# Batch 0 of a fused attention and maxout-FFN kernel: fillers between the turns, and another order for the first loads

## The chip, the cores and the metric

The kernel runs on one core of a Trainium2 chip. The metric is the device time of one execution in microseconds, a median over several executions. The kernel before was run again beside each group of variants, on the same chip. A ratio is the mean time of one kernel's runs over the mean of the other's runs in the same rounds, so it is not quite the ratio of the medians that I quote. Each execution also reports its mean granted TensorE clock.

## The reference, cut to what matters

```python
k_all = np.concatenate([beacon_k, k], axis=2)      # B = H = 8, S = 576, D = 64, 16 beacons
v_all = np.concatenate([beacon_v, v], axis=2)
scores = scale * np.matmul(q, k_all.transpose(0, 1, 3, 2))
scores = np.where(causal, -1000000000.0, scores)
a = softmax(scores)
attn = np.matmul(a, v_all)
x = attn.transpose(0, 2, 1, 3).reshape(B * S, H * D)          # 4608 x 512
h = np.maximum(np.maximum(x @ w1, x @ w2), x @ w3)            # 512 x 768 each
out = h @ w_out
```

## The kernel before

TensorE executes a fixed order of work. A *pair* is two heads, a *quad* four heads; batch 0 has pairs 0 to 3. For each pair q and k are *turned* (transposed on TensorE into PSUM and copied back by VectorE), then scores are computed in four groups, ScalarE takes the exponential, VectorE or GpSimd masks it, and TensorE multiplies it with the values. The FFN is cut into units of matmuls that are interleaved with the attention of the next batch. The first twelve units need weights 1 and 2 only, and the thirteenth is the first that needs weight 3.

The first batch is written out as a list of steps; each entry is a group of scores and what follows it:

```python
first_steps = [
    ((0, 0), [T(2, 0, False)]),                      # T(p, h): turn half h of pair p
    ((1, 0), [T(3, 0, True, None, 4), L(next_load, 2), V(0)]),
    ((2, 0), []),
    ((3, 0), [T(0, 1, False, None, 4), M(0, 0, True), V(1), L(load_w, 0, 0, d_ff), V(2)]),
    ...
    ((0, 2), [T(2, 1, False), M(2, 0, True), M(0, 2), V(3), V(4), L(load_w, 1, 0, d_ff)]),
    ((0, 3), [T(3, 1, False), M(3, 0, True), M(0, 3, True)]),
    ((1, 1), [M(1, 1)]),
    ...
    ((2, 2), [P(1, 0, True, 2, 4), invert_sums, M(2, 2, True), G(0), L(load_wide, n_quad, 1)]),
    ((2, 3), [P(0, 1, False, 0, 2), multiply, M(2, 3), CW(2, 0), L(load_w, 2, 0, d_ff)]),
    ((3, 1), [P(0, 1, False, 2, 4), invert_sums, F(1), M(3, 1, True)]),     # F: one FFN unit
    ...
    ((3, 3), [F(1), M(3, 3, True), CW(2, 1), L(turn_quad, 2, 0), F(1), TW(2, 1, 0), P(1, 1), ...]),
]
```

`load_w(i, ...)` loads weight i + 1 in two pieces, issued by GpSimd, with a cast to bf16 on the way. `G(0)` and `load_wide(n_quad, 1)` load q and k of the first quad of batch 1 through SyncE's queue; G's load waits for a tiny VectorE memset into its buffer, which is how it is held back until VectorE has got that far (in the profile of the kernel before the memset runs at 22.11 us for 0.06 and the load goes out at 22.19). `CW` casts a loaded quad on GpSimd. `keep_busy` and `fill` issue matmuls or transposes whose result nobody reads; they only occupy TensorE:

```python
def fill(ps, n):
    for i in range(n):
        x0 = 512 + 128 * (i % 4)
        nc.tensor.transpose(ps[:, x0 : x0 + 128], busy[:, 0:128], ident)

def keep_busy(n, cols=320, ffn=False):
    ps = ffn_psum.tile([128, 512], FP32, name="fps") if ffn else pv_bank(1, [128, 512], FP32)
    for _ in range(n):
        nc.tensor.matmul(ps[:, 0:cols], busy[:, 0:128], busy[:, 0:cols], start=True, stop=True)
```

The softmax here doesn't subtract the row's maximum and nothing guards it: scores larger than these inputs give would overflow.

Of the kernel before, what the change touches and what calls it, by code (L numbers as in the profile page):

```python
# [16 lines left out]
def kernel(  # L17
# [13 lines left out]
    nc = tc.nc  # L31
# [5 lines left out]
    d_model, d_ff = moe_w1.shape  # L37
# [26 lines left out]
    n_quad = 2  # L64
# [5 lines left out]
    B_PE = 4  # L70
# [71 lines left out]
    bk16_1 = const.tile([NB_PE - Nb, H, D], BF16, name="bk16_1")  # L142
# [21 lines left out]
    def pv_bank(i, shape, dtype):  # L164
        return pv_psum.tile(shape, dtype, name=f"pv{i}")
# [3 lines left out]
    by_pool = nc.gpsimd.tensor_copy  # L169
# [217 lines left out]
    def fill(ps, n):  # L387

        for i in range(n):
            x0 = 512 + 128 * (i % 4)  # L390
            nc.tensor.transpose(ps[:, x0 : x0 + 128], busy[:, 0:128], ident)

    def turn_half(p, h, pv, q_copy=None, idle=0):
        for i in range(2):
            src = stage.pop(("half16", p, h, i))
            if pv:
                bank = pv_bank(i, [128, 1024], BF16)
            else:
                bank = ffn_psum.tile([128, 1024], BF16, name="fps")
            ps = bank[:, 0:HALF]  # L400
            if i == 0:
                fill(bank, idle)
            for r in range(HR):
                for e in range(2):
                    nc.tensor.transpose(
                        ps[64 * e : 64 * e + 64, r * QP : (r + 1) * QP],
                        src[:, e, r],
                        ident[0:QP, 0:QP],
                        tile_position=(0, 64 * e),
                    )  # L410
            x0 = i * Nb + HALF * h
            dst = (qTs, kTs)[i][p % NT][:, x0 : x0 + HALF]
            (q_copy if i == 0 and q_copy else by_dve)(  # L413
                dst.rearrange("d (p r) -> d p r", r=HR), ps.rearrange("d (r p) -> d p r", r=HR)
            )
# [272 lines left out]
    def emit_ffn(limit, pool=None, name="fps"):  # L688
        if done[0] == len(units):
            return False  # L690
        need, fn, args = units[done[0]]
        if done[0] + 1 <= limit + 1e-6 and need <= ready[0]:
            fn(*args, pool or ffn_psum, name)
            done[0] += 1
            return True
        return False
# [5 lines left out]
    def at_step(p, g, *fns):  # L702
        plan.setdefault((p, g), []).extend(fns)

    def L(fn, *a):
        return lambda: fn(*a)
# [3 lines left out]

    def load_qk(b):
        if b < B_PE:
            return [L(load_wide, n_quad * b + g, i) for g in range(n_quad) for i in range(2)]
        return [L(load_pair, p) for p in range(b * PPB, (b + 1) * PPB)]

    loads = [L(load_v, 0, 0, nc.gpsimd), L(load_v, 0, 1, None, (nc.scalar, nc.sync)), L(load_beacons, 1, B_PE, bk32_1)]
    loads += load_qk(1)[2:] + load_v_pieces(1)
    for b in range(2, B):
        if b == B_PE - 1:
            loads.append(L(load_beacons, B_PE, B, bk32))  # L720
        loads += load_qk(b) + load_v_pieces(b)

    def next_load(n=1):
        for _ in range(n):
            if loads:
                loads.pop(0)()

    def C(fn, *a):
        def run():
            fn(*a)  # L730
            next_load()

        return run

    def start():
# [22 lines left out]
        cast_half(0, 1, by_act)  # L758
        by_dve(bk16_0, bk32_0)
        turn_half(0, 0, False, by_act)  # L760
        keep_busy(4)
        turn_beacons(0, 1, bk16_0)
        by_act(qk_all[:, 1:PPB, S : S + Nb], bT[:, 1:PPB, 0:Nb])
        cast_half(1, 0, by_dve)
        cast_half(1, 1, by_dve)
        keep_busy(2)
        turn_half(1, 0, True, by_act)

    pv_at = {}
# [4 lines left out]
    def steps(p):  # L774
        return [[0, 1], [2, 3]]

    def T(p, h, pv, q_copy=None, idle=0):
        def run():
            turn_half(p, h, pv, q_copy, idle)

        return run

    def M(p, gi, dve=False):
        return L(emit_masks, p, gi, dve)

    def P(quad, hf, apart=False, first=0, last=len(passes)):
        return L(emit_pv, quad, hf, first, last, apart)

    def V(t):
        return L(cast_first_v, t)  # L790

    def G(i):
        return L(load_wide, n_quad, i, nc.vector)

    def F(n):
        return lambda: [emit_ffn(END) for _ in range(n)]

    def CW(quad, i):
        return L(cast_wide, quad, i, by_pool)

    def TW(quad, i, n, act=False):
        return L(turn_wide, quad, i, n, by_act if act else by_dve, False)

    def cast_p():
        for g in range(n_quad):
# [6 lines left out]

    first_steps = [
        ((0, 0), [T(2, 0, False)]),
        ((1, 0), [T(3, 0, True, None, 4), L(next_load, 2), V(0)]),
        ((2, 0), []),
        ((3, 0), [T(0, 1, False, None, 4), M(0, 0, True), V(1), L(load_w, 0, 0, d_ff), V(2)]),
        ((0, 1), [T(1, 1, True), M(1, 0, True), M(0, 1)]),
        ((0, 2), [T(2, 1, False), M(2, 0, True), M(0, 2), V(3), V(4), L(load_w, 1, 0, d_ff)]),
        ((0, 3), [T(3, 1, False), M(3, 0, True), M(0, 3, True)]),  # L820
        ((1, 1), [M(1, 1)]),
        ((1, 2), [P(0, 0, False, 0, 2), M(1, 2)]),
        ((1, 3), [P(0, 0, False, 2, 4), invert_sums, M(1, 3, True)]),
        ((2, 1), [P(1, 0, True, 0, 2), multiply, M(2, 1), cast_p]),
        ((2, 2), [P(1, 0, True, 2, 4), invert_sums, M(2, 2, True), G(0), L(load_wide, n_quad, 1)]),
        ((2, 3), [P(0, 1, False, 0, 2), multiply, M(2, 3), CW(2, 0), L(load_w, 2, 0, d_ff)]),
        ((3, 1), [P(0, 1, False, 2, 4), invert_sums, F(1), M(3, 1, True)]),
        ((3, 2), [F(1), multiply, L(turn_beacons, 1, B_PE, bk16_1), L(next_load, 5), M(3, 2, True)]),
        ((3, 3), [F(1), M(3, 3, True), CW(2, 1), L(turn_quad, 2, 0), F(1), TW(2, 1, 0), P(1, 1), invert_sums, TW(2, 1, 1, True),
                  L(place_quad_beacons, 2, by_act), F(1), multiply]),  # L830
    ]
    at_step(4, 0, C(cast_wide, 3, 0, by_pool))
    at_step(4, 1, C(cast_wide, 3, 1, by_pool))
    at_step(5, 0, C(cast_v, 1, 0, by_pool))
    at_step(5, 1, C(cast_v, 1, 1, by_pool))
    at_step(5, 0, L(load_w_out))
# [3 lines left out]
    for b in range(2, B):  # L840
        p = b * PPB
# [6 lines left out]
    for b in range(B_PE, B):  # L848
        p = b * PPB
# [117 lines left out]
```

## Time and profile before

| | kernel before |
|---|---|
| median of the first three runs | 300.07 us (299.07 to 300.17) |
| span of the profiled execution | 298.3 us |
| TensorE busy | 286.5 us |
| TensorE at half clock | 15.73 to 25.97 us |
| first quad of batch 1 requested | 22.19 us |
| first scores of batch 1 | 36.02 us |

Idle time of TensorE is what to look for, since it is busy 96% of the span; but "busy" does not tell at which clock, so the clock row has to be read beside it. The lines themselves stand in the prediction.

### The profile page before, as it was taken

The page shows a single profiled execution, that of the slowest core. Times are in us where ns is not written, and L with a number is a line of the kernel's source. Part 1 is how long each engine was busy: PE and PEld are TensorE (multiplying, and loading weights), DVE is VectorE, ACT ScalarE, POOL GpSimd, SP SyncE. Part 2 cuts the span into 40 slices and gives each one's busy share as a digit, 9 for nine tenths or more (in the row PEclk, how much of TensorE's full clock was granted, in tenths as well). Part 3 has the DMA queues.
Part 4 walks back from the last instruction along what each step waited for, and adds up shares of the span by engine and source line. Part 5 has one row for each costly group of instructions (what it writes and reads, how often), then busy time and mean ns, then how long its engine had stood idle before and what let it go on. Part 6 is the DMA issues. An engine that isn't in the chain of part 4 may idle for free.

```text
span 298.3 us, 8565 instructions
## 1 busy us (share of the span) xinstructions
PE 286.5 (96%) x3548; PEld 153.2 (51%) x3548; DVE 173.8 (58%) x341; ACT 147.3 (49%) x231; POOL 121.7 (41%) x241
## 2 busy tenths in 40 slices
PE   8699899999999999999999999999999999999995
PEld 4446675454545445454545777545454554444442
DVE  3754766456667565646563757375746575284373
ACT  4775488776655455546453646364635431401300
POOL 7282298465446453636454645554233210000000
PEclk9957999999999999999999999999999999999999
DMA  8999999977927999999999899898412001103003
GB/s 146 212 177 322 234 279 270 195 266 203 226 54 206 213 254 224 191 195 239 265 190 237 226 234 223 207 208 201 117 69 79 2 0 73 70 3 122 18 0 141
DMA packets 83589, 50.64 MB, mean 170 GB/s; under 512 B 64224, under 2 KB 75232, under 8 KB 83552
## 3 DMA queue, kind: packets, MB, share of 16 engines
q1 hardware_dynamic: 77904, 45.50, 65.1%
q0 software_dynamic: 4048, 4.03, 8.4%
q10 hardware_dynamic: 1600, 0.59, 1.0%
q8 instruction: 27, 0.44, 0.7%
q14 instruction: 10, 0.08, 0.1%
HBM read 35.13 MB, written 14.22 MB: 165 GB/s over the span
## 4 chain that ended last, share of the span: by engine, by line
PE 87%; DVE 5%; ACT 3%; DMA 2%; issue 1%; POOL 1%; POOLq 0%; DVEq 0%
PE fps L596 32%; PE pv L536 14%; PE sc L596 12%; PE fps L632 11%; PE sc L464 10%; PE sc L632 4%; PE fps L615 2%; DMA quad<-in_k_dram 2%; ACT at_sb L473 1%; PE pv L373 1%; DVE qkT L380 1%; DVE at_sb L490 1%; DVE xT L568 1%; DVE y L640 1%; DVE qkT L413 1%
## 5 line engine op out<-in xcount | busy, mean ns | idle before, releaser
L473 ACT ACTIVATE at_sb<-sc 128x928 bf16<-128x928 f32 (+5 forms) x128 | 104.0, 861 | 88.3 <-PE sc L464 86.5
L596 PE MATMUL fps<-xT,w_sb 128*128 128x512 bf16 (+1 forms) x488 | 110.2, 357 | 0.5 <-DVE xT L568 0.5
L492 POOL TENSOR_SCALAR_AFFINE_SELECT at_sb<-at_sb 128x256 bf16<-128x256 bf16 (+2 forms) x146 | 53.2, 383 | 105.7 <-ACT at_sb L473 105.0
L596 PEld LDWEIGHTS <-w_sb 128*128 128x128 bf16 x672 | 61.6, 98 | 65.0 <-issue 12.0
L606 DVE TENSOR_TENSOR hT<-hT,fps 128x512 bf16<-128x512 bf16 x72 | 49.4, 687 | 34.4 <-PE fps L596 34.4
L596 PE MATMUL sc<-xT,w_sb 128*128 128x512 bf16 (+1 forms) x184 | 42.1, 356 | 0.0
L464 PE MATMUL sc<-qkT 64*128 64x288 bf16 (+5 forms) x400 | 36.6, 284 | 2.3 <-ACT at_sb L473 0.7
L632 PE MATMUL fps<-w_out_sb,hT 128*128 128x512 bf16 x150 | 36.0, 379 | 0.0
L640 DVE COPY y<-fps 128x512 f32<-128x512 f32 x25 | 17.3, 692 | 27.6 <-PE fps L632 24.8
L632 PEld LDWEIGHTS <-hT 128*128 128x128 bf16 x210 | 19.8, 98 | 24.0 <-DVE hT L606 1.9
L536 PE MATMUL pv<-at_sb,v_sb 128*32 128x288 bf16 (+5 forms) x1376 | 30.3, 235 | 0.4 <-issue 0.4
L606 DVE TENSOR_TENSOR hT<-hT,sc 128x512 bf16<-128x512 bf16 x30 | 20.6, 688 | 16.4 <-PE sc L596 16.2
L604 DVE CAST hT<-fps 128x512 bf16<-128x512 f32 x31 | 21.4, 692 | 12.8 <-PE fps L596 12.8
L568 DVE TENSOR_TENSOR xT<-pv,recip 128x288 bf16<-128x288 f32 (+2 forms) x93 | 27.3, 349 | 2.6 <-ACT recip L558 2.6
L464 PEld LDWEIGHTS <-qkT 64*128 64x128 bf16 x400 | 14.4, 95 | 26.3 <-issue 18.9
L536 PEld LDWEIGHTS <-v_sb 128*32 128x32 bf16 (+1 forms) x1408 | 25.4, 99 | 3.9 <-issue 2.2
L248 POOL CAST p<-st 96x768 bf16<-96x768 f32 x32 | 25.5, 823 | 0.0
L287 POOL CAST v_sb<-st 128x1536 bf16<-128x1536 f32 (+2 forms) x21 | 18.4, 895 | 0.0
L536 PE MATMUL pv<-at_sb,ones 128*32 128x288 bf16 (+4 forms) x500 | 17.7, 263 | 0.4 <-DVE qkT L380 0.4
L556 ACT ACTIVATE lnd<-pv 128x288 f32<-128x288 f32 x31 | 12.9, 416 | 8.5 <-PE pv L536 8.5
L237 POOL CAST p<-st 128x1152 bf16<-128x1152 f32 x12 | 13.7, 1143 | 5.1 <-DMA st<-in_q_dram 5.1
L604 ACT CAST hT<-sc 128x512 bf16<-128x512 f32 x6 | 3.5, 585 | 23.7 <-PE sc L596 23.7
(73 smaller groups left out, 173.9 us busy)
## 6 DMA issues: line engine op xcount, KB each, us to landing
out_dram<-y SPq DMA_DIRECT2D x35, 256.0 KB, 2.3
st<-in_v_dram SPq DMA_DIRECT2D x23, 256.0 KB, 6.5
st<-in_q_dram SPq DMA_DIRECT2D x16, 288.0 KB, 4.6
st<-in_k_dram SPq DMA_DIRECT2D x16, 288.0 KB, 5.3
st<-in_q_dram SPq DMA_DIRECT2D x6, 576.0 KB, 6.3
st<-in_k_dram SPq DMA_DIRECT2D x6, 576.0 KB, 6.9
w_sb<-in_moe_w_dram POOLq DMA_DIRECT2D x6, 384.0 KB, 6.6
q_dram<-p SPq DMA_DIRECT2D x16, 144.0 KB, 2.3
```

The costliest lines, as they stand in the source:

```text
L248: cast(part.rearrange("p r h d -> p h r d"), st[0:QP, i * NQ2 : (i + 1) * NQ2].rearrange("p (h r d) -> p h r d", h=2, r=QR),)
L287: cast(v_sb[0:n, t:t1].rearrange("p t h d -> p (t h d)"), st[0:n, (t - t_lo) * H * D : (t1 - t_lo) * H * D],)
L464: nc.tensor.matmul(ps[:, e, off : off + q1 - q0], kT[hs, 128 * t : 128 * t + 128], qT[hs, q0:q1], start=True, stop=True, tile_position=(64 ...
L473: nc.scalar.activation(out=both_heads(p, gi), in_=ps[:, :, 0 : g_width(p, gi)], func=AF.Exp, scale=scale)
L492: nc.gpsimd.affine_select(out=view, in_=view, compare_op=ALU.is_ge, fill=0.0, base=x0, pattern=[[0, 2], [1, hi - lo]], channel_multiplier=-1,)
L536: nc.tensor.matmul(ps[bank][32 * j : 32 * j + 32, lo + q0 - qa : lo + qb - qa], lhsT, at_view(pair_of(quad, j)[0], t, pair_of(quad, j)[1], ...
L568: nc.vector.tensor_mul(xT[:, 2 * g + part - 1, c0 + ca : c0 + cb], ps[bank][:, lo : lo + cb - ca], recip[:, ca:cb],)
L596: nc.tensor.matmul(ps[:, o0 : o0 + n], w_in[i][:, ct, 128 * ft : 128 * (ft + 1)], xT[:, ct, x0 : x0 + n], start=(ct == 0), stop=(ct == n_c ...
L604: (by_act if alone[0] else by_dve)(h, ps)
L606: nc.vector.tensor_max(h, h, ps)
L632: nc.tensor.matmul(ps, hT[:, ft, 128 * tt : 128 * (tt + 1)], w_out_sb[:, ft, :], start=(ft == 0), stop=(ft == n_ft - 1),)
L640: nc.vector.tensor_copy(y, ps)
```

## The change

Its intent, as far as the code tells it: spread a few fillers over the gaps between the turns so that TensorE's clock stays up; move the last turn of pair 3 behind the scores (1,1); ask for the first quad of batch 1 two groups of scores sooner and ahead of weight 2; hold the second quad back until VectorE has passed a certain mask; and request weight 3 last, behind the casts of the second quad. The core of the diff:

```diff
-            if i == 0:
-                fill(bank, idle)
+            fill(bank, idle[i])
...
-            return [L(load_wide, n_quad * b + g, i) for g ... for i in range(2)]
+            return [L(load_wide, n_quad * b + g, i, nc.vector if (b, g, i) == (1, 1, 0) else None) for g ... for i in range(2)]
...
-        ((2, 0), []),
+        ((2, 0), [L(keep_busy, 1, 320, True)]),
...
+        ... V(2), L(keep_busy, 1)]),                                   # end of (3, 0)
-        ((0, 2), [T(2, 1, False), M(2, 0, True), M(0, 2), V(3), V(4), L(load_w, 1, 0, d_ff)]),
-        ((0, 3), [T(3, 1, False), M(3, 0, True), M(0, 3, True)]),
-        ((1, 1), [M(1, 1)]),
+        ((0, 2), [T(2, 1, False, None, (0, 3)), M(2, 0, True), M(0, 2), V(3), V(4)]),
+        ((0, 3), [M(0, 3, True), L(keep_busy, 1)]),
+        ((1, 1), [T(3, 1, False), M(3, 0, True), M(1, 1)]),
...
+        ((1, 3), [..., M(1, 3, True), G(0), L(load_wide, n_quad, 1)]),
+        ((2, 1), [..., M(2, 1), L(load_w, 1, 0, d_ff), cast_p]),
-        ((2, 2), [..., M(2, 2, True), G(0), L(load_wide, n_quad, 1)]),
-        ((2, 3), [..., M(2, 3), CW(2, 0), L(load_w, 2, 0, d_ff)]),
...                                          # in (3, 3): TW(2, 1, 0) now ahead of the FFN unit
-    at_step(4, 1, C(cast_wide, 3, 1, by_pool))
+    at_step(4, 1, C(cast_wide, 3, 1, by_pool), L(load_w, 2, 0, d_ff))
```

More of the change, by code (lines that the diff above doesn't have):

```diff
@@ L391, in fill, with turn_half @@
             nc.tensor.transpose(ps[:, x0 : x0 + 128], busy[:, 0:128], ident)
-    def turn_half(p, h, pv, q_copy=None, idle=0):
+    def turn_half(p, h, pv, q_copy=None, idle=(0, 0)):
         for i in range(2):
@@ L712, in load_qk @@
         if b < B_PE:
-            return [L(load_wide, n_quad * b + g, i) for g in range(n_quad) for i in range(2)]
+            return [L(load_wide, n_quad * b + g, i, nc.vector if (b, g, i) == (1, 1, 0) else None) for g in range(n_quad) for i in range(2)]
         return [L(load_pair, p) for p in range(b * PPB, (b + 1) * PPB)]
@@ L775, in steps, with T @@
         return [[0, 1], [2, 3]]
-    def T(p, h, pv, q_copy=None, idle=0):
+    def T(p, h, pv, q_copy=None, idle=(0, 0)):
         def run():
@@ L814 @@
         ((0, 0), [T(2, 0, False)]),
-        ((1, 0), [T(3, 0, True, None, 4), L(next_load, 2), V(0)]),
-        ((2, 0), []),
-        ((3, 0), [T(0, 1, False, None, 4), M(0, 0, True), V(1), L(load_w, 0, 0, d_ff), V(2)]),
+        ((1, 0), [T(3, 0, True, None, (4, 0)), L(next_load, 2), V(0)]),
+        ((2, 0), [L(keep_busy, 1, 320, True)]),
+        ((3, 0), [T(0, 1, False, None, (4, 0)), M(0, 0, True), V(1), L(load_w, 0, 0, d_ff), V(2), L(keep_busy, 1)]),
         ((0, 1), [T(1, 1, True), M(1, 0, True), M(0, 1)]),
-        ((0, 2), [T(2, 1, False), M(2, 0, True), M(0, 2), V(3), V(4), L(load_w, 1, 0, d_ff)]),
-        ((0, 3), [T(3, 1, False), M(3, 0, True), M(0, 3, True)]),
-        ((1, 1), [M(1, 1)]),
+        ((0, 2), [T(2, 1, False, None, (0, 3)), M(2, 0, True), M(0, 2), V(3), V(4)]),
+        ((0, 3), [M(0, 3, True), L(keep_busy, 1)]),
+        ((1, 1), [T(3, 1, False), M(3, 0, True), M(1, 1)]),
         ((1, 2), [P(0, 0, False, 0, 2), M(1, 2)]),
-        ((1, 3), [P(0, 0, False, 2, 4), invert_sums, M(1, 3, True)]),
-        ((2, 1), [P(1, 0, True, 0, 2), multiply, M(2, 1), cast_p]),
-        ((2, 2), [P(1, 0, True, 2, 4), invert_sums, M(2, 2, True), G(0), L(load_wide, n_quad, 1)]),
-        ((2, 3), [P(0, 1, False, 0, 2), multiply, M(2, 3), CW(2, 0), L(load_w, 2, 0, d_ff)]),
+        ((1, 3), [P(0, 0, False, 2, 4), invert_sums, M(1, 3, True), G(0), L(load_wide, n_quad, 1)]),
+        ((2, 1), [P(1, 0, True, 0, 2), multiply, M(2, 1), L(load_w, 1, 0, d_ff), cast_p]),
+        ((2, 2), [P(1, 0, True, 2, 4), invert_sums, M(2, 2, True)]),
+        ((2, 3), [P(0, 1, False, 0, 2), multiply, M(2, 3), CW(2, 0)]),
         ((3, 1), [P(0, 1, False, 2, 4), invert_sums, F(1), M(3, 1, True)]),
-        ((3, 2), [F(1), multiply, L(turn_beacons, 1, B_PE, bk16_1), L(next_load, 5), M(3, 2, True)]),
-        ((3, 3), [F(1), M(3, 3, True), CW(2, 1), L(turn_quad, 2, 0), F(1), TW(2, 1, 0), P(1, 1), invert_sums, TW(2, 1, 1, True),
+        ((3, 2), [F(1), multiply, L(turn_beacons, 1, B_PE, bk16_1), M(3, 2, True), L(next_load, 5)]),
+        ((3, 3), [F(1), M(3, 3, True), CW(2, 1), L(turn_quad, 2, 0), TW(2, 1, 0), F(1), P(1, 1), invert_sums, TW(2, 1, 1, True),
                   L(place_quad_beacons, 2, by_act), F(1), multiply]),
```

## The prediction

What (a) calls a filler net of the drain is measured in the kernel before: one filler of 320 columns at full clock lasts 0.299 us and two together 0.45, so the second adds 0.15 (these are the warm ones; the twelve ahead of 4.4 us last 0.474 each, in the median); one filler transpose lasts 0.22 and four 0.40, so each further one adds 0.06. That the fillers would keep the clock was my estimate from the busy times of the windows. The windows are 3.41 us long, a third of the two measured stretches of 10.24. The "near 400 GB/s" of (f) is the 392 of the last window; that weight 3 would share that rate was an estimate.

> **What bounds the kernel now.** I read the page first, for busy shares and clock. Its columns are forty slices of 7.46 us, in tenths.
>
> ```profile
> PE 286.5 (96%) x3548; PEld 153.2 (51%) x3548; DVE 173.8 (58%) x341; ACT 147.3 (49%) x231; POOL 121.7 (41%) x241
> ...
> PE   8699899999999999999999999999999999999995
> ...
> PEclk9957999999999999999999999999999999999999
> DMA  8999999977927999999999899898412001103003
> ```
>
> TensorE is the bound: 286.5 of 298.3 us busy, so only 12 us idle, and the waits of TensorE after 36 us list nothing above 0.7 us in total. Work that TensorE gets through earlier at the start should therefore come off the end. The change touches only the first 45 us. There the page shows two faults: a second slice with 6 tenths busy, and a third and fourth slice whose clock is 5 and 7 tenths.
>
> Second, I read windows cut where the clock changes (us, busy time by engine, clock, DMA share, GB/s):
>
> ```profile
> 5.49:8.90 3.41, 2.79 (x48) 1.66 (x47) 2.36 (x7) 1.98 (x6) 0.54 (x1) 1.00 1.44 201
> 8.90:12.31 3.41, 2.44 (x48) 1.53 (x48) 1.89 (x6) 2.96 (x3) 0.61 (x1) 1.00 1.40 185
> 12.31:15.73 3.42, 2.36 (x46) 1.54 (x48) 3.30 (x13) 2.32 (x3) 2.08 (x4) 1.00 1.33 229
> 15.73:19.14 3.41, 3.41 (x58) 1.51 (x54) 2.17 (x8) 2.62 (x4) 2.88 (x7) 0.50 1.06 194
> 19.14:22.55 3.41, 3.41 (x64) 1.59 (x66) 1.24 (x6) 2.74 (x5) 2.30 (x6) 0.50 1.00 170
> 22.55:25.97 3.42, 3.42 (x78) 2.29 (x71) 0.89 (x3) 1.93 (x4) 0.33 (x1) 0.50 1.00 249
> 25.97:29.38 3.41, 3.41 (x34) 2.22 (x32) 2.15 (x6) 2.12 (x5) 0.72 (x1) 1.00 1.04 392
> ```
>
> The clock falls to one half at 15.73 us and returns at 25.97: 10.24 us. Before the fall TensorE was busy 2.79, 2.44 and 2.36 us per 3.41 us, falling; then, at half clock, it is busy all the time and everybody waits for it.
>
> Third, I read the timelines of each engine around the hand-over to batch 1 (28 to 36 us) and before the fall:
>
> ```profile
> 14.12 0.32 PE L405 MATMUL fps<-ident,quad 96*64 96x96 bf16 x6 [0.68 <-DMA quad<-in_k_dram]
> ...
> 14.99 0.68 PE L405 MATMUL fps<-ident,quad 96*64 96x96 bf16 x12 [0.33 <-DVE qkT L413]
> 15.61 0.83 PE L464 MATMUL sc<-qkT 64*128 64x288 bf16 x8
> ...
> 22.19 0.39 SPq L189 DMA_DIRECT2D st<-in_q_dram  x1
> ...
> 28.66 1.14 POOL L237 CAST p<-st 128x1152 bf16<-128x1152 f32 x1 [5.06 <-DMA st<-in_q_dram]
> 29.74 1.08 POOL L309 DMA_DIRECT2D w_sb<-in_moe_w_dram  x2
> ...
> 30.42 1.66 DVE L490 TENSOR_TENSOR at_sb<-at_sb,tri 128x160 bf16<-128x160 bf16 x1
> 30.81 1.16 POOL L237 CAST p<-st 128x1152 bf16<-128x1152 f32 x1
> ...
> 32.03 0.45 PE L373 MATMUL fps<-ident,p 128*128 128x128 bf16 x5 [0.62 <-POOL p L237]
> ...
> 36.02 0.54 PE L464 MATMUL sc<-qkT 64*128 64x288 bf16 x8 [0.27 <-ACT qkT L424]
> ```
>
> The first quad of batch 1 is asked for at 22.19, GpSimd waits 5.06 us for it, casts q, issues weight 3 (1.08 us), and casts k only then; TensorE's turn of k waits for that cast. From the third FFN unit's end (29.39 in the timeline of TensorE) to the first scores of batch 1 (36.02) are 6.63 us, with 0.47 + 0.62 + 0.39 + 0.27 = 1.75 us of TensorE idle.
>
> [...]both stretches of 10.24 us are three times 3.41 us and the clock is 1.00 or 0.50. [...]eight filler transposes of before did not prevent the fall. [...]the mask at 30.42 takes 1.66 us, where its line's median is 0.27, and ends at 32.08, just after the cast at 30.81 + 1.16 = 31.97.[...]
>
> **The change part by part.** (a) Fillers. Added are three matmuls of 320 columns and three transposes of 128. Two warm 320-column fillers took 0.45 us together in the timeline, so about 0.14 us each net of the drain; four transposes took 0.40, about 0.06 each. Sum 3 x 0.14 + 3 x 0.06 = 0.6 us, all of it put where TensorE was idle (0.46 before the scores at 10.38, 0.43 before 11.92, 0.68 before 14.12, 0.3 before 14.99): cost near zero. Benefit: of the window 12.31 to 15.73, one matmul and three transposes, 0.32 us, or 9% of the window; from 2.36 to some 2.7 us, near the 2.79 of a window that did not cause a fall. I take three chances in four that the fall at 15.73 does not come.
>
> (b) Turn of pair 3 moved behind the scores (1,1). These scores stood behind a turn that waited until 14.99; they can now start when ScalarE has left the bank, about 14.8 instead of 15.61. ScalarE's exponential then begins about 15.4 instead of 16.16: 0.8 us sooner.
>
> (c) Full clock from 15.7. TensorE's 10.24 us there would be 5.1, but ScalarE then becomes the bound. I add its work from scores (1,1) to the start of (3,3): exponentials 0.98 + 0.78 + 0.65 + 0.98 + 0.78 + 0.65 + 1.00 + 0.78 = 6.6, three pairs of logarithm and reciprocal 3 x 0.85 = 2.55, together 9.15 us from 15.4: 24.55, and TensorE's third FFN unit, whose scores come just before, ends near 25.9 (two units of 1.0 behind exponentials, with 0.3 of scores between). Before it ended at 29.39. Gain 3.5 us of the 5.1, (b) included.
>
> (d) First quad. It is asked for after the mask of (1,3), which follows the exponential ending near 17.8: about 18.3 instead of 22.19. It landed 6.3 (q) and about 7.4 us (k) after its request; so q at 24.6 and k at 25.7 at worst, and weight 2, now issued near 20, does not run ahead of it. Casts of 1.14 and 1.16 us end near 26.9 at the latest. With k's two casts back to back (no 1.08 us of issue between), k's turn before the FFN unit and no blocked mask, I remove 1.4 of the 1.75 us of idle. Sum (b) to (d): 3.5 + 1.4 = 4.9 us.
>
> (e) Second quad gated. Asked for near 25.6 instead of 23.14. Landing times of 8 to 10 us become at most 35; its first turn was at 40.76, about 36 when shifted. Cost 0.
>
> (f) Weight 3 last. Its issue goes behind the cast that began at 40.29 and took 1.14, so about 41.43 - 4.9 = 36.5, two issues of 0.55. Weight loads took 5.1 to 9.1 us: both pieces there between 43.4 and 46.2. The first matmul with it ran at 48.08, shifted 43.2. A stall of 0 to 3 us; as it shares with wide loads at near 400 GB/s, I take 0.5.
>
> Net 4.9 - 0.5 = 4.4 us: 300.07 - 4.4 = 295.7.
>
> **The rivals.** First, the clock falls all the same, there or a window later[...]. For it: eight filler transposes did not help before, and TensorE now gets idle time behind ScalarE. Against: the window at 29.4 to 32.8 was busy about 2.0 us only and did not cause a fall. Then only 1.4 us of (d) stays: 298.7. Second, weight 3 comes too late and TensorE stands 2 to 3 us at about 43: 297.5 to 298. Against: fewer transfers stand ahead of it. Third, TensorE, not ScalarE, remains the limit from 15.7, so the whole 5.1 us is saved and all 1.75 of idle go: 300.07 - 6.85 = 293.2. Against: ScalarE's own sum of 9.15 us leaves no room for it. Fourth, DMA is the bound of the first 60 us (share 1.0 and more) and the gain is given back in waits for values. Against: after 45 us GpSimd's casts waited 0.2 us for loads.
>
> **Range and chances.** Clock kept and weight 3 in time or nearly: 294 to 297, about 70%. Clock lost or weight 3 late: 297 to 299.3, about 22%. Under 294 about 6%. More than 2% is a gain of 6.0 us, which only the third rival gives: 0.1. Slower by 2% would need a second fall of the clock: 0.02.
>
> **What would show it.** Right: clock 1.00 in the stretches from 15.7 to 26 and TensorE with waits on ScalarE there; the first quad's request near 18.3; GpSimd's wait of 5.06 us below 2; the mask of 1.66 us gone; first scores of batch 1 near 31; the time after that stage unchanged. Wrong: any slice before 45 us with a clock of one half, or first matmuls with weight 3 behind an idle time ended by the weight's DMA of over 1 us.

## The result, and the profile after

The changed kernel took 303.53 us (302.45 to 303.91, four runs) against 300.06 us of the kernel before: a ratio of 1.0117, interval 1.0083 to 1.0151. It is 1.2% slower; I had predicted 295.7 us.

From the page of the changed kernel, engine busy shares and then the clock in forty slices of 7.55 us:

```profile
PE 286.6 (95%) x3554; PEld 153.1 (51%) x3554; DVE 173.6 (58%) x342; ACT 147.3 (49%) x231; POOL 121.7 (40%) x241
...
PE   8887995999999999999999999999999999999995
...
PEclk9999997799999999999999999999999999999999
```

The dip of the clock in the third and fourth slice has gone, as predicted. But there is a new hole: slice 7 of TensorE shows 5 tenths, and slices 7 and 8 show a clock of 7 tenths. The windows of the changed kernel (us, busy time of PE, PEld, DVE, ACT and POOL with instruction counts, clock, DMA share, GB/s) put numbers to it:

```profile
15.73:25.97 10.24, 8.65 (x211) 5.38 (x207) 5.75 (x19) 7.81 (x14) 7.05 (x14) 1.00 1.02 241
...
45.73:49.15 3.42, 1.04 (x6) 0.15 (x6) 1.48 (x4) 1.75 (x3) 3.27 (x7) 1.00 1.08 262
49.15:52.56 3.41, 2.27 (x13) 1.45 (x14) 1.20 (x2) 0.24 (x1) 0.04 (x1) 0.50 1.21 201
52.56:55.97 3.41, 3.41 (x40) 1.56 (x42) 0.91 (x2) 1.83 (x3) 0.29 (x1) 0.50 1.24 232
```

Between 45.73 and 49.15 us TensorE is busy for 1.04 us only, and then the clock is at one half for 6.83 us. The timelines of the changed kernel say why (start, duration, engine, line, what; in brackets the idle time ahead and what ended it):

```profile
18.66 0.38 SPq L189 DMA_DIRECT2D st<-in_q_dram  x1
...
28.00 1.15 POOL L237 CAST p<-st 128x1152 bf16<-128x1152 f32 x1 [2.22 <-DMA st<-in_k_dram]
...
29.20 0.45 PE L373 MATMUL fps<-ident,p 128*128 128x128 bf16 x5 [1.12 <-POOL p L237]
...
33.61 0.54 PE L463 MATMUL sc<-qkT 64*128 64x288 bf16 x8 [0.27 <-ACT qkT L423]
...
38.96 1.08 POOL L309 DMA_DIRECT2D w_sb<-in_moe_w_dram  x2
...
46.71 0.60 PE L595 MATMUL fps<-xT,w_sb 128*128 128x512 bf16 x2 [0.54 <-DMA w_sb<-in_moe_w_dram]
50.29 1.03 PE L595 MATMUL fps<-xT,w_sb 128*128 128x512 bf16 x2 [2.97 <-DMA w_sb<-in_moe_w_dram]
```

The first scores of batch 1 come at 33.61 instead of 36.02: up to there the change gains 2.41 us. Weight 3 is issued at 38.96 and 39.50. Its first piece is there at 46.71, its second only at 50.29, so TensorE stands 0.54 + 2.97 = 3.51 us. By then the clock has fallen, and two matmuls of 512 columns take 1.03 us where the two ahead of the wait took 0.60.

After that no further difference shows in the times. The same group of scores, which follows a wait of 0.24 us about a quarter through the run, first in the kernel before and then in the changed one:

```profile
71.62 0.55 PE L464 MATMUL sc<-qkT 64*128 64x288 bf16 x8 [0.24 <-DVE qkT L380]
```

```profile
75.17 0.55 PE L463 MATMUL sc<-qkT 64*128 64x288 bf16 x8 [0.24 <-DVE qkT L380]
```

That is 3.55 us later, and the spans differ by 301.8 - 298.3 = 3.5 us. I call this group the *marker*; the whole effect is decided ahead of it. The sum closes: from the first scores of batch 1 to the marker the kernel before takes 71.62 - 36.02 = 35.60 us, the changed one 75.17 - 33.61 = 41.56, which is 5.96 more. The wait is 3.51 of it. The time at half clock with work to do, 50.29 to 55.97, is 5.68 us and costs, by an estimate from the granted clock of 0.50, half of that, 2.84. The kernel before has a gap of 0.39 us in this stretch that the changed one has not. 3.51 + 2.84 - 0.39 = 5.96, and 5.96 - 2.41 = 3.55.

### The profile page after: what moved, and what is told of

The parts are those of the page before. It is cut to its first block, busy times and chain, and to the rows that moved or that the text cites. A ratio compares the mean times of both kernels' runs of the same rounds, so it can differ in the third digit from the quotient of the medians.

```text
span 301.8 us, 8581 instructions
## 1 busy us (share of the span) xinstructions
PE 286.6 (95%) x3554; PEld 153.1 (51%) x3554; DVE 173.6 (58%) x342; ACT 147.3 (49%) x231; POOL 121.7 (40%) x241
## 4 chain that ended last, share of the span: by engine, by line
PE 82%; DMA 8%; DVE 4%; POOL 2%; ACT 2%; issue 1%; SPq 0%; POOLq 0%; DVEq 0%
PE fps L595 32%; PE sc L595 12%; PE pv L535 12%; PE fps L631 11%; PE sc L463 8%; PE sc L631 4%; DMA w_sb<-in_moe_w_dram 4%; DMA st<-in_k_dram 3%; DMA quad<-in_k_dram 2%; PE pv L373 1%; POOL p L237 1%; ACT at_sb L472 1%; DVE y L639 1%; DVE qkT L412 1%; DVE xT L567 1%
## 5 line engine op out<-in xcount | busy, mean ns | idle before, releaser
L595 PE MATMUL fps<-xT,w_sb 128*128 128x512 bf16 (+1 forms) x488 | 111.7, 360 | 4.0 <-DMA w_sb<-in_moe_w_dram 3.5
L535 PE MATMUL pv<-at_sb,v_sb 128*32 128x288 bf16 (+5 forms) x1376 | 29.1, 229 | 1.6 <-issue 1.6
L535 PEld LDWEIGHTS <-v_sb 128*32 128x32 bf16 (+1 forms) x1408 | 24.5, 96 | 4.0 <-issue 2.2
```

Source lines behind the costliest of these rows:

```text
L535: nc.tensor.matmul(ps[bank][32 * j : 32 * j + 32, lo + q0 - qa : lo + qb - qa], lhsT, at_view(pair_of(quad, j)[0], t, pair_of(quad, j)[1], ...
L595: nc.tensor.matmul(ps[:, o0 : o0 + n], w_in[i][:, ct, 128 * ft : 128 * (ft + 1)], xT[:, ct, x0 : x0 + n], start=(ct == 0), stop=(ct == n_c ...
```

## The experiments

Theory A was that weight 3's late landing, with the fall of the clock that it causes, is the loss. Its rivals: that something else would take its place (the gated second quad, the moved turn), and that the fillers or the earlier quad do not do what the first 34 us seem to show. Twelve runs in three groups, each group on one chip; all gave the reference's output. The last two columns are from each variant's one profile.

| run | what it is | median us | before beside it | ratio, 95% interval | mean clock, by run | first scores of batch 1 | marker |
|---|---|---|---|---|---|---|---|
| e1 | changed, weight 3 early | 301.18 | 300.41 | 0.9975 (0.9888 to 1.0062) | .975 .994 .989 1.0 | 38.71 | 74.04 |
| e2 | before, weight 3 last | 301.68 | 300.41 | 1.0023 (0.9962 to 1.0085) | .976 .981 .981 .994 | 35.74 | 72.38 |
| e3 | before, fillers only | 300.52 | 300.41 | 0.9996 (0.9917 to 1.0076) | .993 .971 .992 .994 | 37.41 | 72.64 |
| e4 | changed, TensorE kept busy in the wait | 301.84 | 300.41 | 1.0008 (0.9930 to 1.0086) | .977 .981 .997 .986 | 35.93 | 74.64 |
| e5 | changed, unedited | 302.00 | 300.14 | 1.0073 (1.0035 to 1.0110) | .998 .988 .994 1.0 .992 | 33.41 | 72.03 |
| e6 | changed, weight 3 in the middle | 300.21 | 300.14 | 1.0008 (0.9965 to 1.0050) | 1.0 .989 .998 .999 .993 | 32.82 | 69.30 |
| e7 | e6, more fillers | 299.95 | 300.14 | 1.0000 (0.9965 to 1.0035) | 1.0 .992 .987 .999 1.0 | 34.49 | 70.75 |
| e8 | e6, without the added fillers | 300.50 | 300.14 | 1.0020 (0.9987 to 1.0053) | .983 .977 .971 .977 .982 | 33.91 | 71.19 |
| e9 | e6, second quad not gated | 301.07 | 299.60 | 1.0059 (1.0027 to 1.0091) | .992 .987 .988 .992 .989 .993 | 36.60 | 71.88 |
| e10 | e6, weight 2 sooner | 301.63 | 299.60 | 1.0071 (1.0035 to 1.0106) | .989 .994 .989 .981 .983 .982 | 38.45 | 73.54 |
| e11 | e7, weight 2 sooner | 301.92 | 299.60 | 1.0048 (1.0002 to 1.0094) | .988 .998 .994 .993 .988 .987 | 37.58 | 72.96 |
| e12 | e6 again | 299.47 | 299.60 | 0.9986 (0.9957 to 1.0014) | .997 .994 .997 .993 .992 .994 | 32.84 | 68.82 |

The kernel before reached a mean clock of 0.969 to 0.988 in the 27 runs beside these.

### Weight 3 early (e1)

```diff
-    at_step(4, 1, C(cast_wide, 3, 1, by_pool), L(load_w, 2, 0, d_ff))
+    at_step(4, 1, C(cast_wide, 3, 1, by_pool))
-        ((2, 3), [..., M(2, 3), CW(2, 0)]),
+        ((2, 3), [..., M(2, 3), CW(2, 0), L(load_w, 2, 0, d_ff)]),
```

> The changed kernel with one thing undone: weight 3 is requested again where the kernel before does it, before the cast of the first quad's k. Theory A (the loss is weight 3's late landing: 0.54 + 2.97 us of TensorE idle in front of its first matmuls, and the clock at one half for the 6.83 us after it, worth about 2.9 us): both go, 303.5 - 3.5 - 2.9 = about 297.1 us, clock 1.00 throughout. Rival B (the loss comes from the gated second quad or the moved turns, weight 3 only happens to be the last to wait): another wait takes its place near 46 to 50 us and the time stays above 301 us.

The wait on weight 3 is gone, which is what theory A says, but the time is 301.18 us and not 297.1; the three fast runs took 298.19 to 301.38 us. The only profile is of the run that is slow (302.74 us), so what follows is an indication and no more. In it the clock fell at 16.00 for 10.24 us, and GpSimd waits for the first quad's k:

```profile
26.44 1.08 POOL L309 DMA_DIRECT2D w_sb<-in_moe_w_dram  x2
31.48 1.14 POOL L237 CAST p<-st 128x1152 bf16<-128x1152 f32 x1 [3.96 <-DMA st<-in_k_dram]
```

Weight 3 is issued while k is still under way, and k's cast waits 3.96 us (2.22 in the changed kernel). The one run of the four with a clock of 1.00 took 298.19 us. The early place of weight 3 seems not to be free either; e6 takes a third place.

### Only weight 3 last, on the kernel before (e2)

```diff
-        ((2, 3), [..., M(2, 3), CW(2, 0), L(load_w, 2, 0, d_ff)]),
+        ((2, 3), [..., M(2, 3), CW(2, 0)]),
-    at_step(4, 1, C(cast_wide, 3, 1, by_pool))
+    at_step(4, 1, C(cast_wide, 3, 1, by_pool), L(load_w, 2, 0, d_ff))
```

> The kernel before with only weight 3 moved to its late place. Theory A: issue near 41.4 and 42, first use at 48.1; with the 7.7 and 10.7 us of landing of the changed kernel the pieces arrive near 49 and 52.7, so TensorE stands 3 to 5 us and the clock falls again afterwards (2 to 3 us): 304 to 308 us. Rival B: without the gated quad the queues are free enough, no wait on weight 3 over 1 us, 300 us.

From its timelines of GpSimd and TensorE:

```profile
41.09 1.08 POOL L309 DMA_DIRECT2D w_sb<-in_moe_w_dram  x2
...
48.23 0.61 PE L596 MATMUL fps<-xT,w_sb 128*128 128x512 bf16 x2
50.16 0.60 PE L596 MATMUL fps<-xT,w_sb 128*128 128x512 bf16 x2 [1.33 <-DMA w_sb<-in_moe_w_dram]
```

The wait is there with this part alone, but only 1.33 us, and the clock does not fall after it. I had expected 3 to 5 us and 304 us or more, so theory A holds in kind and was too large in size; the ratio of 1.0023 shows no loss of time. It is not that TensorE asks for the weight later here. The request moves with the demand: issue and first use are 41.09 and 48.23, 7.14 us apart; in the changed kernel TensorE would have been ready at 45.65 + 0.51 = 46.16, that is 7.20 us after its issue at 38.96. What differs is the landing. The second piece took 10.74 us from its issue in the changed kernel and 8.5 us here, 2.2 us less, and the stalls, 3.51 and 1.33, differ by 2.18. So the late place is costly when the load is slow. Why it is slower beside the other parts of the change is not shown.

### Only the fillers, on the kernel before (e3)

```diff
-        ((2, 0), []),
+        ((2, 0), [L(keep_busy, 1, 320, True)]),
...                                    # as in the change: (3, 0), and T(2, 1, False, None, (0, 3))
-        ((0, 3), [T(3, 1, False), M(3, 0, True), M(0, 3, True)]),
+        ((0, 3), [L(keep_busy, 1), T(3, 1, False), M(3, 0, True), M(0, 3, True)]),
```

> The kernel before with the fillers alone (same three matmuls and three transposes; the order of loads and turns as before, so one filler stands ahead of the last turn). Theory A (fillers keep the clock): clock 1.00 from 15.7 to 26 us; the third FFN unit ends about 2 us sooner, the first quad is requested about 2 us sooner since its gate follows TensorE's work, total 297.5 to 298.5 us. Rival C (the moved turn, not the fillers, kept the clock): clock 0.50 for about 10 us as before and 300 us.

The profiled run has a mean clock of 0.993, and before the wait below its FFN units take 1.05 us for eight matmuls (at 23.73 and 25.04), as those of the kernel before do at full clock (1.04 and 1.05 at 30.37 and 28.34). Ten us at half clock, as in the kernel before (0.983), would not leave 0.993, so in this run the fillers alone did keep the clock; rival C falls for it. The time is 300.52 us all the same, where I had expected 297.5 to 298.5. From its timelines of SyncE's queue, GpSimd and TensorE:

```profile
20.18 0.38 SPq L189 DMA_DIRECT2D st<-in_q_dram  x1
...
29.88 1.14 POOL L237 CAST p<-st 128x1152 bf16<-128x1152 f32 x1 [7.87 <-DMA st<-in_q_dram]
...
31.08 1.14 PE L373 MATMUL pv<-ident,p 128*128 128x128 bf16 x9 [4.99 <-POOL p L237]
```

TensorE reaches the end of its third unit at 26.09 and then stands 4.99 us for the first quad. The quad was asked for 2.0 us sooner than in the kernel before (20.18 against 22.19), but its q was cast 1.2 us later (29.88 against 28.66): the load took 9.7 us and not 6.5. Behind that wait the clock is down: the eight matmuls of the next unit, at 32.01, take 1.91 us instead of 1.05. The whole gain is given back in one wait. One of its four runs had a mean clock of 0.971, so the clock was down for longer in that one; where it fell is not recorded, as only one run has a profile.

### TensorE kept busy while it waits for weight 3 (e4)

```diff
     def mm1_unit(tb, ft, i, pool, name):
+        if (tb, ft, i) == (0, 0, 2):
+            keep_busy(24, 320, True)
```

> The changed kernel with 24 more filler matmuls of 320 columns (about 3.3 us) directly ahead of the first matmul with weight 3, inside the time in which TensorE waits for it. It measures the clock's part by itself: the wait for weight 3 ends when it did (near 50.3 us), but the clock should not fall. Theory A: 303.5 - 2.9 = about 300.6 us, clock 1.00 after 49 us. If the fall of the clock costs nothing, 303.5 us; if the fillers push the chain, over 304 us.

Its timeline of TensorE: the first scores of batch 1, the first matmuls with weight 3, and the marker:

```profile
35.93 0.54 PE L463 MATMUL sc<-qkT 64*128 64x288 bf16 x8 [0.27 <-ACT qkT L423]
...
48.43 3.43 PE L431 MATMUL fps<-busy 128*128 128x320 bf16 x24
51.70 1.32 PE L597 MATMUL fps<-xT,w_sb 128*128 128x512 bf16 x4
...
74.64 0.55 PE L463 MATMUL sc<-qkT 64*128 64x288 bf16 x8 [0.24 <-DVE qkT L380]
```

The clock stays at 1.00 after 49 us, as expected. But in this execution it had already fallen at 12.00 for 13.65 us, so everything came 2.3 us later than in the changed kernel (first scores at 35.93, not 33.61), and the total, 301.84 us where I had expected 300.6, does not measure the fall by itself. The stretch from the first scores to the marker does, since the clock is 1.00 over all of it: 74.64 - 35.93 = 38.71 us, against 41.56 in the changed kernel, 2.85 less. The wait is nearly the same: the second pair of matmuls with weight 3 starts 4.43 us after the last scores ahead of it (47.99 to 52.42), there 4.64 (45.65 to 50.29). That leaves 2.85 - 0.21 = 2.64 us for the fall of the clock, where the sum above gave it 2.84.

### The changed kernel again (e5)

No edit.

> The changed kernel unedited, on the chip of the three runs beside it, as their yardstick. Theory A: again one long wait on weight 3 (2 to 4 us of TensorE idle near 46 to 51 us) and a fall of the clock at its end; mean clock 0.985 to 0.994 in most runs, 302.5 to 304 us. If the first chip was at fault, no such wait and under 300 us.

```profile
47.07 0.60 PE L595 MATMUL fps<-xT,w_sb 128*128 128x512 bf16 x2 [1.10 <-DVE xT L567]
49.81 0.60 PE L595 MATMUL fps<-xT,w_sb 128*128 128x512 bf16 x2 [2.14 <-DMA w_sb<-in_moe_w_dram]
...
72.03 0.55 PE L463 MATMUL sc<-qkT 64*128 64x288 bf16 x8 [0.24 <-DVE qkT L380]
```

On another chip the wait is there again, 1.10 + 2.14 = 3.24 us (the profile names VectorE for the first part, but in the first profile of the changed kernel the same place waits for the weight). In this execution, the fastest of the five, the clock (mean 0.998) did not fall after it, which I had expected it to: the two matmuls behind the wait take 0.60 us, as those ahead of it. It reached the marker at 72.03, 38.62 us after the first scores of batch 1, where the first profile of the same kernel took 41.56. The difference is 2.94 us, of which 3.51 - 3.24 = 0.27 is the wait and 2.67 the clock, which agrees with e4's 2.64. Behind a wait of 3.51 us the clock fell in the first profile, behind one of 3.24 it did not here.

### Weight 3 in the middle (e6, and again as e12)

```diff
-    at_step(4, 1, C(cast_wide, 3, 1, by_pool), L(load_w, 2, 0, d_ff))
+    at_step(4, 1, C(cast_wide, 3, 1, by_pool))
-        ((3, 3), [F(1), M(3, 3, True), CW(2, 1), L(turn_quad, 2, 0), ...
+        ((3, 3), [F(1), M(3, 3, True), CW(2, 1), L(load_w, 2, 0, d_ff), L(turn_quad, 2, 0), ...
```

> The changed kernel with weight 3 requested directly behind the cast of the first quad's k, some 9 us sooner than in the changed kernel and behind k's landing instead of ahead of it. Theory A: no wait on weight 3, and k's load is not delayed by it as it was when weight 3 was early (10.96 us); a profile with clock 1.00 gives 297 to 298 us, one with a fall near 12 or 16 us about 300. Against the changed kernel 4 to 6 us less. Rival B (something else near 46 us takes its place): over 301 us.

> Weight 3 in the middle, unedited, as the yardstick of the three beside it and a second sample of its spread: 298 to 301 us, median within 0.5 us of 299.8; mean clock 0.99 to 1.00.

From the timeline of TensorE of e6:

```profile
28.90 0.83 PE L614 MATMUL fps<-xT,w_sb 128*128 128x256 bf16 x6 [1.42 <-DMA w_sb<-in_moe_w_dram]
32.82 0.55 PE L463 MATMUL sc<-qkT 64*128 64x288 bf16 x8 [0.27 <-ACT qkT L423]
...
44.03 0.56 PE L535 MATMUL pv<-at_sb,ones 128*32 128x176 bf16 x7 [0.84 <-POOL at_sb L491]
...
69.30 0.55 PE L463 MATMUL sc<-qkT 64*128 64x288 bf16 x8 [0.24 <-DVE qkT L380]
```

Issued at 26.01, weight 3 makes nobody wait. The marker comes at 69.30 (e12: 68.82), 2.3 to 2.8 us ahead of the kernel before and 2.7 to 6.4 ahead of the two profiles of the changed kernel. Beside it on one chip the changed kernel took 302.00 and e6 300.21 us: 1.8 us less, where I had expected 4 to 6. Theory A stands, and moving this one request takes back most of the loss; the clearer evidence for it is the marker and the wait that is gone, since the intervals of the two ratios overlap a little. (e6's profile is of its fastest run; e12's is of a more usual one.)

But e6 does not beat the kernel before: 1.0008 and 0.9986, both intervals around 1. Two things are seen that eat into the gain. First, with weight 3 out of the way two other loads are waited for: 1.42 us for the second piece of weight 2 at 28.90, and 0.84 us at 44.03, where GpSimd stood 0.82 us for the values of batch 1, which are behind the gated second quad. Second, executions differ by up to 4.4 us (297.89 to 302.32). One source is the clock (0.989 to 1.000), another the end: in e12's profile the last two stores landed 4.2 and 4.0 us after their issue, where in e6's and in the kernel before's they took 2.0 and 1.8. That profile is 2.8 us ahead at the marker and 0.5 us at the end of the span.

### More fillers (e7), and none of the added ones (e8)

```diff
 # e7, on top of e6
-        ((0, 0), [T(2, 0, False)]),
+        ((0, 0), [T(2, 0, False, None, (0, 4))]),
...                                    # (0, 3) becomes (0, 6); keep_busy 1 becomes 2; T(3, 1) gets (3, 0)
-        ((3, 1), [..., invert_sums, F(1), M(3, 1, True)]),
+        ((3, 1), [..., invert_sums, L(keep_busy, 6, 320, True), F(1), M(3, 1, True)]),
 # e8, on top of e6
-        ((2, 0), [L(keep_busy, 1, 320, True)]),
+        ((2, 0), []),
...                                    # and the other two keep_busy and the (0, 3) out
```

> As weight 3 in the middle, with more fillers: 4 transposes in the first wait for k (7.7 us), 3 more at the turn near 13.5, one matmul more near 14.5, 3 transposes at the moved turn and 6 matmuls in front of the first FFN unit, where TensorE stood. Theory D ([...]the changed kernel's fillers leave too little margin): the clock is 1.00 in all or nearly all runs and the spread between runs shrinks, 296.5 to 298 us. If falls come as often as without them, the fillers are not what decides and the times are those of weight 3 in the middle.

> As weight 3 in the middle, with the changed kernel's six added fillers taken out again (the moved turn stays). Theory C (fillers keep the clock in 12 to 16 us): the clock falls for 7 to 14 us in most runs, mean clock 0.975 to 0.988, 299.5 to 301.5 us. Rival (the moved turn is enough): mean clock and time as with fillers.

Without the added fillers all five runs have a mean clock of 0.971 to 0.983, as the kernel before has; with them e6 has 0.989 to 1.000 in the same rounds. The two ranges do not touch, so the fillers keep the clock and the moved turn alone does not. The window ahead of the fall in e8's profile, and the one after it:

```profile
11.28:14.69 3.41, 2.31 (x44) 1.37 (x45) 3.15 (x13) 2.09 (x4) 1.15 (x3) 1.00 1.33 238
14.69:18.11 3.42, 3.42 (x66) 1.64 (x62) 2.71 (x10) 2.72 (x5) 2.42 (x5) 0.50 1.13 176
```

What a kept clock is worth is another matter: 300.21 against 300.50 us, not distinguishable; in the profiles the first scores of batch 1 come at 32.82 against 33.91. More than the change's six fillers gives nothing (299.95 us, clocks of 0.987 and 0.992 still occur): theory D falls.

### The second quad not gated (e9) and weight 2 sooner (e10, e11)

```diff
 # e9, on top of e6
-            return [L(load_wide, ..., i, nc.vector if (b, g, i) == (1, 1, 0) else None) ...
+            return [L(load_wide, ..., i) ...
-        ((1, 3), [..., G(0), L(load_wide, n_quad, 1)]),
+        ((1, 3), [..., G(0), L(load_wide, n_quad, 1), L(next_load, 2)]),        # and 3 instead of 5 in (3, 2)
 # e10, on top of e6; e11 the same on top of e7
-        ((0, 2), [..., V(3), V(4)]),
+        ((0, 2), [..., V(3), V(4), L(load_w, 1, 0, d_ff)]),
-        ((2, 1), [..., M(2, 1), L(load_w, 1, 0, d_ff), cast_p]),
+        ((2, 1), [..., M(2, 1), cast_p]),
```

> Weight 3 in the middle, with the gate on the second quad taken away and its request put directly behind the first quad's, so that it and the values of batch 1 behind it go out near 20 us as the queue allows. Theory E (the loads of the first 45 us are the bound: what is asked for sooner only makes something else later): the first quad's k or weight 2 lands 1 to 3 us later, TensorE waits that much longer near 28 us, and the wait of 0.84 us for batch 1's values near 43 us goes; total within 1 us of the ungated twin. If the gate were the cause of the lost gain, 2 us or more faster than it.

> Weight 3 in the middle, with weight 2 requested where the kernel before does (behind the last cast of batch 0's values, near 19 us, not after the mask of (2,1) near 20.5). Theory E: the wait of 1.42 us on weight 2's second piece near 28 us shrinks to under 0.7 us and k's cast comes later by up to 1 us; first scores of batch 1 within 0.7 us of 32.8, total within 1 us. If weight 2's place were worth what the change hoped, 1 to 3 us slower.

> The candidate: weight 2 sooner, weight 3 in the middle, more fillers. If both small gains add and the clock is kept, 297.5 to 299 us, 0.5 to 1% under the kernel before; if the loads bind, 299 to 300 us.

The timeline of TensorE of e9, then of e10:

```profile
31.20 1.46 PE L614 MATMUL fps<-xT,w_sb 128*128 128x256 bf16 x6 [2.42 <-DMA w_sb<-in_moe_w_dram]
```

```profile
31.62 0.71 PE L373 MATMUL fps<-ident,p 128*128 128x128 bf16 x5 [4.30 <-POOL p L237]
```

Theory E (the loads are the bound, so what is asked for sooner makes something else later) fits what e9 and e10 measured and was too modest in size. The edit of e9 does two things: it removes the gate, and it asks for the second quad directly behind the first, so the two can't be told apart. In it weight 2 is issued sooner than in e6 (19.57 against 20.45) and yet comes later (the matmuls that wait for its second piece start at 31.20, in e6 at 28.90), and TensorE waits 0.74 + 2.42 us for it instead of 1.42; 301.07 against e12's 299.47 us on the same chip. In e10 weight 2 is issued at 19.08 instead of 20.45, and the first quad's k comes later: from request to cast it took 11.3 us, where e6 took 6.8. TensorE waits 4.30 us for that cast; 301.63 against 299.47 us. Behind the wait the clock is down: in e9 twenty matmuls with the ones take 1.15 us at 32.59 (0.68 in e6), in e10 the eight matmuls of an FFN unit take 1.91 at 32.13 (1.05 at 25.13), and in e11 four transposes take 0.61 at 36.08 (0.40 in e6). So these two parts of the change, the gate with the second quad's later place and the first quad's place ahead of weight 2, do help: about 1.6 and 2.2 us, once weight 3 is not in the way. The candidate e11 is not distinguishable from either.

## Why the prediction was wrong, point by point

**The clock and the fillers** (a): right. The clock from 15.7 to 26 us is 1.00, and e8 against e6 (mean clocks of 0.971 to 0.983 against 0.989 to 1.000) shows that it is the fillers' doing. They don't hold it in every execution: e4's profile has the same fillers there and a fall at 12.00.

**The moved turn** (b): right. The scores of (1,1) start at 14.68, said 14.8.

**ScalarE as the bound to the third FFN unit** (c): the number came near, by luck; the mechanism was wrong. The third unit ends at 24.38 + 1.05 = 25.43 us in e12, said 25.9. But TensorE did not wait for ScalarE there: in e12 it works from 15.33 to the third unit with a single idle time above 0.1 us, 0.16, and the chain that ended last is TensorE alone from 15.4 to 22.9. So TensorE stayed the limit, as my third rival had it. What kept its 10.24 us from becoming 5.1 is that its work did not halve at full clock. From the first matmuls with values to the first FFN unit the kernel before takes 16.36 to 25.66 = 9.30 us at half clock, e12 15.60 to 21.83 = 6.23 us. The same twelve matmuls in both, 19.91 - 19.24 = 0.67 us and 17.93 - 17.48 = 0.45 us apart:

```profile
19.24 0.74 PE L536 MATMUL fps<-at_sb,ones 128*32 128x288 bf16 x12
19.91 0.74 PE L536 MATMUL fps<-at_sb,v_sb 128*32 128x288 bf16 x12
```

```profile
17.48 0.51 PE L535 MATMUL fps<-at_sb,ones 128*32 128x288 bf16 x12
17.93 0.52 PE L535 MATMUL fps<-at_sb,v_sb 128*32 128x288 bf16 x12
```

In the changed kernel's own profile the third unit ends at 26.26 + 1.05 = 27.31. Of the 1.9 us between it and e12, some 1.4 are one gap of TensorE from 22.00 to 23.56, inside the last matmuls with the values. The profile names nothing that it waited for; e5 has 1.28 and e9 0.94 us at the same place, e6 0.25 and e12 0.16. What causes it stays open.

**The first quad** (d): mis-sized. Asked for at 18.66 (said 18.3), but k's own request is the second of the two and goes out at 19.08, and k took 8.9 us to land, not 7.4. So its cast began at 28.00, where I had k landed "at 25.7 at worst". Of the 1.4 us of idle that I removed, the changed kernel saved 0.33: from the third unit to the first scores are 33.61 - 27.31 = 6.30 us, before 6.63. Two of its signs failed with it: GpSimd still waited 2.50 us for q and 2.22 for k, not below 2, and the slow mask of 1.66 us still took 1.03 (at 28.21), beside the cast of k. Together (b) to (d) gave 2.41 us and not 4.9; with weight 3 in the middle 3.2.

**The gate** (e): I gave it no cost and no gain. e9 shows a gain of about 1.6 us, for the gate and the second quad's later place together, in the mended kernel.

**Weight 3 last** (f): this is the step that failed. I gave it "a stall of 0 to 3 us", took 0.5, and it measured 3.51, followed by 2.84 by the sum (2.64 and 2.67 by e4 and e5) for the fall of the clock, which I had left out altogether, although in my own reading of the kernel before the window with 2.36 us of work in 3.42 was followed by half clock. The term that was mis-sized is the landing. The demand was about right: from issue to need I had 43.2 - 36.5 = 6.7 us, and it was 7.2. But the second piece took 10.74 us from its issue (39.50 to 50.24 in the chain of waits), where the longest I had seen was 9.1. Even with weight 3's own landings in the kernel before, 7.5 and 9.1 us, the second piece would have come at 46.2 against a need at 43.2, a stall of 3.0 us; taking 0.5 leaned on loads of 5.1 us. (With 5.1 us the second piece would come at 37.05 + 5.1 = 42.2; the lower end of 43.4 that I wrote does not follow.) I named the wait as my second rival, with 297.5 to 298 us; it became the result, with its clock, at 303.5. The miss of 7.8 us is, in the profiles' terms, 3.0 of wait, 2.8 of clock and 2.5 of missing gain in (b) to (d), less the gap of 0.4 that went.

**The fourth rival**, loads as the bound of the first 60 us, I dismissed because GpSimd's casts waited 0.2 us for loads after 45 us. That slack was measured in a kernel whose TensorE was slow up to 36 us. The runs show that such slack does not carry over, because the landing time itself changed from one order of requests to another: in e3 the first quad, asked for 2.0 us sooner, took 9.7 us instead of 6.5; in e10 the first quad's k took 11.3 us instead of 6.8; in e9 weight 2 was issued sooner than in e6 and came later.

That what differs after the first stage reaches the end unchanged was right: 3.55 us at the marker, 3.5 in the span. One slip of the chances: a gain of more than 2% (6.0 us, so 294.1 or less) got 0.1, while the range under 294 got 6%.

## What to carry to other kernels

The time from a load's request to its landing is not a constant of that load: the second piece of weight 3 took 9.1, 8.5 and 10.7 us in three kernels. So it isn't enough to shift request and first use by the same gain, as I did. Before moving a request, list what will be under way beside it, take the longest landing seen rather than a middle one, and if several loads then come short, count the loads as the bound and not the engine. A wait on TensorE can cost more than its length: here 3.51 us of wait, with the fall of the clock, cost 6.35 by the sum, while behind the 1.33 us of e2 and the 3.24 of e5 the clock did not fall. When one request is moved to make room for another, look for a place between "in the way" and "too late", and judge by a fixed marker in the trace, as executions of one kernel here differ by more than the effect.

The busy time of a window did not tell by itself whether the clock would fall behind it: windows of 3.41 us with 2.36 (12.31 us in the kernel before), 2.31 (11.28 in e8) and 2.43 us busy (8.59 in e4) were followed by half clock, windows with 2.44 and 2.01 us (8.90 and 29.38 in the kernel before) were not. What decides it is not shown. Nor was the rate of the loads one figure: with a DMA share near 1 (1.03, 0.95 and 0.99), the kernel before moved 391 GB/s from 26 to 30 us, in packets of 2.2 KB on average, e6 187 GB/s from 36 to 42 us, where the values are under way, and 190 from 24.28 to 27.70, where weight 2 is.
